# A second PSUM tile for the scores of batch 1, and batch 1 spread over one more H item, in a windowed attention followed by an MLP

## The chip, the cores and the metric

The kernel runs on one core of one Trainium2 chip. The metric is the device time in microseconds of one execution. A core has five engines that work side by side, each through its own list of instructions in order: PE (TensorE, matrix products and transposes into PSUM), ACT (ScalarE), DVE (VectorE), POOL (GpSimd) and SP (SyncE, which here only issues DMAs). [...] a matrix product writes a bank, and ACT or DVE must have read it before PE writes it again. An instruction that waits holds up everything behind it on its engine.

## The reference

Eight batches of eight heads with 576 positions and head size 64 go through causal attention with a window of 128 and an ALiBi bias; the heads are put side by side to 4608 tokens of 512, which go through two matrix products with a swish between them.

```python
scores = scale * np.matmul(q, k.transpose(0, 1, 3, 2))      # q, k, v: (8, 8, 576, 64)
mask = (rel >= 0) & (rel < 128)
scores = np.where(mask, scores + bias[None], -1000000000.0)
scores = scores - np.max(scores, axis=-1, keepdims=True)
attn = np.exp(scores)
attn = attn / (np.sum(attn, axis=-1, keepdims=True) + 1e-09)
attn_out = np.matmul(attn, v)
x = attn_out.transpose(0, 2, 1, 3).reshape(B * S, H * D)    # (4608, 512)
h = x @ w_in                                                # w_in: (512, 2048)
g = h * (1.0 / (1.0 + np.exp(-beta * h)))
out = g @ w_out                                             # w_out: (2048, 512)
```

## The kernel before, in words

**The steps of attention.** For a batch b, the first 512 positions of q and k are loaded for a pair of heads p and cast to bf16 by POOL (`load_pair`, line 113). `TP(b, p, i)` transposes q (i = 0) or k (i = 1) of that pair with four PE instructions (L224) into a `psum_t` bank, and DVE copies it to `QK` (L228). `TT(b)` does the same for the last 64 positions (L237, L242). `SC(b, m, p)` is a score step for one pair: it takes a PSUM tile of two banks, for batches 0 and 1 writes the bias into it with two products (L262), adds four (m = 0) or six (m = 1) products of q and k (L276), and ACT takes exp of the whole tile (L284). From batch 2 on the bias sits in four exps (L289) and DVE multiplies with a mask (L293); the masks and the exps' bias column are made by `late_consts` (L195, L200). `PV(b, qb, g)` multiplies the weights of query block qb and four heads g with v (L316, L320) and DVE divides by the sum (L325 reciprocal, L326 multiply). `X(b, qb)` transposes the finished 128 tokens with four PE instructions (L344), and ACT copies them into `XT`, the input of the MLP (L348); from batch 3 on a DMA does this.

**The steps of the MLP.** Tokens are taken in nine groups g of 512. `HS(g, j)`, an H item, is four products for 128 of the 2048 hidden columns (L360); ACT takes tanh (L365) and DVE makes `gT` of it (L366). `OS(g, i, n)` adds four of the sixteen products of an output block (L376), and after the last ACT scales it (L391) and a DMA stores it.

**PSUM.** `psum_s` holds one score tile (two banks), `psum_t` two banks for transposes, PV and X. In the first stage `psum_x` has the other four as two more score tiles. Then `psum_h` and `psum_o` take two banks each. `psum_o` is O's: it holds the output blocks, the first of which comes after H group 1. Before that it serves some H items and some PV steps.

**The order.** PE's order is written out by hand. Batch 0 runs first, then H group 0 begins: items 0 and 1, X(0, 4), items 2 to 7. Then `spread` lays all steps of batch 1 (`by_pair(1)`) evenly between items 8 to 13, in the order of that list: after each H item as many steps as its share of the cost. Items 14 and 15 with X(1, 2) and X(1, 3) follow, then batch 2's first transposes and group 1. The other engines follow PE's order as the framework places them; from group 1 on the orders of SP and POOL are fixed too. W1 (`moe_w_in`) comes in four chunks of 512 columns, so that H item 8 is the first that needs the third chunk and item 12 the first that needs the fourth.

```python
s1 = by_pair(1) + [pv(1, 3, 1)]
spread(h0[8:14], s1, 0, [(6, len(s1))])
h0[14]()
X(1, 2)
h0[15]()
X(1, 3)
```

Of the kernel before, what the change touches and what calls it, by code (L numbers as in the profile page):

```python
# [12 lines left out]
F32 = mybir.dt.float32  # L13
P = 128
# [3 lines left out]
def kernel(  # L18
# [10 lines left out]
    nc = tc.nc  # L29
# [12 lines left out]
    NQB = 5  # L42
    ROWS = [P, P, P, P, 64]
    NDM = DM // P
    NFF = DFF // P
# [28 lines left out]
    XT = const.tile([P, NDM, XTR], BF16, name="XT")  # L74
# [11 lines left out]
    psum_s = ctx.enter_context(tc.tile_pool(name="psum_s", bufs=1, space=bass.MemoryType.PSUM))  # L86
# [123 lines left out]
    def idle(to, n):  # L210

        for _ in range(n):
            nc.tensor.matmul(
                to, lhsT=zero[:, 0:P], rhs=zero[:], start=True, stop=True, skip_group_check=True
            )
# [4 lines left out]
    def TP(b, p, i):  # L220
        src = staged[b, p]
        tps = psum_t.tile([P, LA, P], BF16, name="tps", tag="t")
        for a in range(LA):
            nc.tensor.transpose(  # L224
                out=tps[:, a, :], in_=src[:, i, a, :, :].rearrange("r h d -> r (h d)"),
                identity=ident[:],
            )
        nc.vector.tensor_copy(  # L228
            out=QK[b % 2][:, i, p, 0:LM].rearrange("c (r a) -> c r a", a=LA),
            in_=tps[:].rearrange("c a r -> c r a"),  # L230
        )
# [100 lines left out]
    def X(b, qb):  # L332
        nq = ROWS[qb]
        xnv = xns.pop((b, qb))[:].rearrange("p h d -> p (h d)")
        tok0 = (b * S + P * qb) % XTR
        n1 = min(nq, XTR - tok0)
        parts = [(tok0, 0, n1)] + ([(0, n1, nq)] if n1 < nq else [])
        if b >= NTE:
            for at, r0, r1 in parts:
                nc.sync.dma_start_transpose(out=XT[:, :, at : at + r1 - r0], in_=xnv[r0:r1, :])  # L340
            return
        xt = psum_t.tile([P, NDM, P], BF16, name="xt", tag="t")
        for c in range(NDM):
            nc.tensor.transpose(  # L344
                out=xt[:, c, :], in_=xnv[:, c * P : (c + 1) * P], identity=ident[:]
            )
        for at, r0, r1 in parts:
            nc.scalar.copy(out=XT[:, :, at : at + r1 - r0], in_=xt[:, :, r0:r1])  # L348


    gts, opss = {}, {}

    def HS(g, j):
        if j == 0:
            gts[g] = gt_pool.tile([P, NFF, TOKG], BF16, name="gT", tag="gT")
        c0 = (g * TOKG) % XTR
        pool, tag = (psum_o, "ops") if j % 2 and j < (6, NFF - 1, 0)[min(g, 2)] else (psum_h, "hps")
        hps = pool.tile([P, TOKG], F32, name="hps", tag=tag)
        for c in range(NDM):
            nc.tensor.matmul(  # L360
                hps[:], lhsT=W1[:, c, bass.ts(j, P)], rhs=XT[:, c, c0 : c0 + TOKG],
                start=(c == 0), stop=(c == NDM - 1),
            )
        sig = sig_pool.tile([P, TOKG], BF16, name="sig", tag="sig")
        nc.scalar.activation(out=sig[:], in_=hps[:], func=ACTF.Tanh, scale=beta_h[:, j : j + 1])  # L365
        nc.vector.scalar_tensor_tensor(  # L366
            out=gts[g][:, j, :], in0=sig[:], scalar=1.0, in1=hps[:], op0=ALU.add, op1=ALU.mult
        )
# [73 lines left out]
    def step(f, c):  # L442
        cost[f] = c
        return f
# [5 lines left out]
        return step(lambda: TT(b), 1)  # L450

    def sc(b, m, p):
        return step(lambda: SC(b, m, p), 2)

    def pv(b, qb, g):

        pool = (psum_o, "ops") if b == 1 and (qb + g) % 2 and qb < 4 else None
        return step(lambda: PV(b, qb, g, pool), 1)

    def x(b, qb):  # L460
        f = step(lambda: X(b, qb), int(b < NTE))
        at[b, qb] = f
        if b >= NTE:
            lazy.append(f)
        return f

    at, lazy = {}, []
# [58 lines left out]
    with tc.manual_schedule(engines={mybir.EngineType.PE}):  # L526

        for sb in range(NQB):
            c = load_v(0, sb)()
            if sb in (1, 3):  # L530
                with tc.issue_after(c.ins):
                    for n in ((0,), (1, 2))[sb // 2]:
                        load_w1(n)
        for p in range(NP):
            c = load_pair(1, p, None if p else VS[0][0:1, NQB - 1, 0, 0:1])
            if p == 1:
                with tc.issue_after(c.ins):
                    load_w1(3)
                load_tail(1)
        for sb in range(NQB):  # L540
            c = load_v(1, sb)()
            if sb == 3:
                with tc.issue_after(c.ins):
                    for n in range(4):
                        load_w2(n)
        with tc.tile_pool(name="psum_x", bufs=2, space=bass.MemoryType.PSUM) as psum_x:
            pools = [psum_x, psum_s, psum_x]

            def sc0(m, p, fill=0):
                SC(0, m, p, pools[0], fill)  # L550
                pools.append(pools.pop(0))

            w = psum_t.tile([P, 512], F32, name="w", tag="t")
            idle(w[:], 9)
            TP(0, 0, 0)
            TP(0, 0, 1)
            sc0(0, 0, 3)
            load_beta()
            TP(0, 1, 0)
            TP(0, 1, 1)  # L560
            sc0(0, 1, 2)
            TT(0)
            TP(0, 2, 0)
            sc0(1, 0, 1)
            TP(0, 2, 1)
            sc0(1, 1)
            TP(0, 3, 0)
            sc0(0, 2)
            TP(0, 3, 1)
            sc0(1, 2)  # L570
            PV(0, 0, 0)
            sc0(0, 3)
            PV(0, 1, 0)
            sc0(1, 3)
            for qb in (2, 3):
                PV(0, qb, 0)
        psum_h = ctx.enter_context(
            tc.tile_pool(name="psum_h", bufs=2, space=bass.MemoryType.PSUM))
        psum_o = ctx.enter_context(
            tc.tile_pool(name="psum_o", bufs=2, space=bass.MemoryType.PSUM))  # L580
        w = psum_s.tile([P, 2, 512], F32, name="w", tag="sps")
        for qb in range(NQB - 1):
            c = PV(0, qb, 1, (psum_o, "ops") if qb % 2 else (psum_h, "hps"))
            idle(w[:, 0, :], 1)
            if qb:
                X(0, qb - 1)
                idle(w[:, 1, :], 1)
        X(0, NQB - 2)
        for g in range(2):
            c = PV(0, NQB - 1, g)  # L590
        with tc.issue_after(c.ins):
            late_consts()
        for p in range(NP):
            load_pair(2, p)
            if p == 1:
                load_tail(2)

        def hs(g):
            return [lambda j=j: HS(g, j) for j in range(NFF)]


        h0, at0 = hs(0), x(0, 4)
        for it in h0[0:2] + [at0] + h0[2:8]:
            it()
        s1 = by_pair(1) + [pv(1, 3, 1)]
        spread(h0[8:14], s1, 0, [(6, len(s1))])
        h0[14]()
        X(1, 2)
        h0[15]()
        X(1, 3)  # L610

        s2 = by_pair(2)
        for f in s2[0:2]:
            f()
        steps, first = [pv(1, 4, 1)] + s2[2:5] + [x(1, 4)] + s2[5:] + [x(2, 2)], {}
        for b in range(NTE, B):
            first[b] = len(steps)
            steps += by_block(b)
        steps += [pv(B - 1, 2, 1), x(B - 1, 2), pv(B - 1, 3, 1), x(B - 1, 3), pv(B - 1, 4, 1),
                  x(B - 1, 4)]  # L620
        with tc.manual_schedule(engines={mybir.EngineType.SP, mybir.EngineType.Pool}):

            early = [(0, 0), (1, 0), (0, 1), (1, 1), (0, 2), (1, 2)]
            late = [(0, 3), (1, 3)] + [(i, n) for i in (2, 3) for n in range(4)]

            def os(g, order):
                return [lambda i=i, n=n: OS(g, i, n) for i, n in order]

            todo, goals = merge(steps, first), []
            moe = hs(1) + os(0, early + late) + os(1, early)  # L630
            for g in range(2, NTG):
                b, r = divmod(TOKG * (g + 1) - 1, S)
                goals.append((len(moe) - 10, todo.index(at[b, r // P]) + 1))
                o = os(g - 1, late) + (os(g, early) if g < NTG - 1 else [])
                h = hs(g)
                moe += sum(([h[n]] + o[n : n + 1] for n in range(NFF)), [])
            spread(moe, todo, 2, goals)
            while stores:
                flush()
            for it in os(NTG - 1, early + late):  # L640
                it()
# [30 lines left out]
```

## Time and profile before

| | before |
|---|---|
| median of 8 executions | 338.62 us (337.82 to 339.56) |
| the profiled execution, its own time | 339.56 us |
| its span, first to last instruction | 337.4 us |
| PE busy | 319.2 us, 95% of the span |
| ACT busy | 215.8 us, 64% |
| DVE busy | 192.2 us, 57% |
| POOL busy | 107.0 us, 32% |
| tensor clock granted | 1.00 of full speed |
| DMA | 48.26 MB, mean 143 GB/s |

The times in the profile count from the first instruction of the profiled execution. A row of the timeline or of the instruction groups names start, busy time, engine, source line, operation and the tiles written and read; the bracket at its end tells how long the engine sat idle before it and what ended that wait. A row of the waits gives the total, the number of times and the longest one. Consecutive instructions of one engine overlap a little, so the start-to-start distance, not the busy time, is what one more of them costs.

### The profile page before, as it was taken

What the parts mean: (1) busy time and instruction counts of PE and PEld (TensorE: products, weight loads), DVE (VectorE), ACT (ScalarE), POOL (GpSimd) and SP (SyncE); (2) the same over time, 40 slices, a digit from 0 to 9 for tenths busy, and PEclk for the clock granted to TensorE, in tenths of its full rate; (3) what the DMA queues carried; (4) which work ended last, traced back from release to release, by engine and by line L of the source; (5) the groups of instructions that cost most, each with busy time, mean ns of one, the idle gap of its engine ahead of it and who ended that gap; (6) DMA issues with size and microseconds to landing.
All of it is one profiled execution on the core that took longest, in us unless ns stands there. A gap on an engine that the chain in (4) does not pass through costs nothing.

```text
span 337.4 us, 6166 instructions
## 1 busy us (share of the span) xinstructions
PE 319.2 (95%) x2240; PEld 152.3 (45%) x2283; DVE 192.2 (57%) x412; ACT 215.8 (64%) x417; POOL 107.0 (32%) x173
## 2 busy tenths in 40 slices
PE   8987787999999999999999999999999999999895
PEld 3453344444544444444444444444444444444342
DVE  6676756797435575656666665566656455344500
ACT  5755466697647876776687757776676664354611
POOL 7742592273553434524243243520100001010000
PEclk9999999999999999999999999999999999999999
DMA  8999989999999999899989788990402012110011
GB/s 199 247 174 243 213 212 234 225 185 170 224 209 213 137 190 182 192 137 201 141 193 176 141 134 183 191 148 12 102 31 64 1 64 62 39 64 31 32 64 62
DMA packets 138638, 48.26 MB, mean 143 GB/s; under 512 B 125664, under 2 KB 136176, under 8 KB 138608
## 3 DMA queue, kind: packets, MB, share of 16 engines
q1 hardware_dynamic: 108208, 32.19, 51.2%
q0 software_dynamic: 30224, 15.54, 33.9%
q8 instruction: 18, 0.29, 0.4%
q10 hardware_dynamic: 176, 0.14, 0.1%
q14 instruction: 12, 0.10, 0.1%
HBM read 36.71 MB, written 9.44 MB: 137 GB/s over the span
## 4 chain that ended last, share of the span: by engine, by line
PE 83%; DMA 7%; DVE 3%; ACT 2%; SPq 1%; issue 1%; POOL 0%
PE ops L376 37%; PE hps L360 34%; PE sps L276 5%; DMA W<-in_moe_w_in_dram 4%; PE pv L320 2%; PE pv L316 2%; DMA fst<-in_k_dram 2%; DMA fst<-in_v_dram 2%; DVE gT L366 1%; PE sps L262 1%; SPq L109 1%; ACT pt L284 1%; ACT sig L365 1%; PE tps L224 1%; DVE qkT L228 1%
## 5 line engine op out<-in xcount | busy, mean ns | idle before, releaser
L360 PE MATMUL hps<-XT,W 128*128 128x512 bf16 x555 | 143.6, 379 | 4.9 <-DMA W<-in_moe_w_in_dram 2.2
L365 ACT ACTIVATE sig<-hps,beta_h 128x512 bf16<-128x512 f32 x144 | 99.2, 692 | 71.9 <-PE hps L360 64.3
L376 PE MATMUL ops<-W,gT 128*128 128x512 bf16 x558 | 142.5, 379 | 1.2 <-issue 0.3
L366 DVE SCALAR_TENSOR_TENSOR gT<-sig,hps 128x512 bf16<-128x512 bf16 x144 | 98.2, 683 | 54.3 <-ACT sig L365 53.6
L289 ACT ACTIVATE pt<-sps,bias 128x256 bf16<-128x256 f32 (+1 forms) x192 | 75.1, 479 | 10.4 <-PE sps L276 10.3
L360 PEld LDWEIGHTS <-W 128*128 128x128 bf16 x576 | 52.1, 98 | 62.0 <-issue 5.0
L376 PEld LDWEIGHTS <-gT 128*128 128x128 bf16 x576 | 51.2, 97 | 55.7 <-issue 2.1
L293 DVE TENSOR_TENSOR pt<-pt,mask 128x1024 bf16<-128x1024 bf16 x48 | 35.5, 740 | 43.9 <-ACT pt L289 43.9
L394 POOL DMA_DIRECT2D out_dram<-osb x32 | 17.9, 560 | 130.1 <-ACT osb L391 130.1
L129 POOL CAST bst<-fst 128x512 bf16<-128x512 f32 (+1 forms) x50 | 31.7, 645 | 42.2 <-DMA fst<-in_q_dram 30.7
L326 DVE TENSOR_TENSOR xn<-pv,zs 128x256 bf16<-128x256 f32 (+1 forms) x80 | 33.6, 422 | 2.3
L391 ACT ACTIVATE osb<-ops 128x512 f32<-128x512 f32 x35 | 21.0, 601 | 18.1 <-PE ops L376 18.0
L320 PE MATMUL pv<-vs,pt 128*128 128x65 bf16 x320 | 28.1, 193 | 0.0
L320 PEld LDWEIGHTS <-pt 128*128 128x128 bf16 x320 | 21.5, 97 | 10.2 <-issue 0.9
L276 PE MATMUL sps<-qkT 64*128 64x256 bf16 (+2 forms) x320 | 25.2, 252 | 0.5 <-DVE qkT L228 0.2
L325 DVE RECIPROCAL zs<-pv 128x4 f32<-128x4 f32 (+1 forms) x80 | 13.8, 174 | 19.4 <-PE pv L320 19.2
L316 PE MATMUL pv<-vs,pt 128*128 128x65 bf16 x256 | 23.5, 193 | 0.6 <-ACT XT L348 0.5
L284 ACT ACTIVATE pt<-sps 128x1024 bf16<-128x1024 f32 x16 | 16.4, 1024 | 11.8 <-PE sps L276 11.4
L276 PEld LDWEIGHTS <-qkT 64*128 64x128 bf16 x320 | 10.4, 94 | 27.8 <-issue 26.3
L316 PEld LDWEIGHTS <-pt 128*128 128x128 bf16 x256 | 19.8, 98 | 6.7 <-issue 0.7
L137 POOL DMA_DIRECT2D vs<-in_v_dram x25 | 21.4, 859 | 0.9 <-issue 0.5
L113 POOL CAST bst<-fst 128x512 bf16<-128x512 f32 x24 | 14.6, 621 | 19.7 <-DMA fst<-in_q_dram 12.9
(47 smaller groups left out, 113.2 us busy)
## 6 DMA issues: line engine op xcount, KB each, us to landing
fst<-in_q_dram SPq DMA_DIRECT2D x32, 256.0 KB, 4.6
fst<-in_k_dram SPq DMA_DIRECT2D x32, 256.0 KB, 5.1
out_dram<-osb POOLq DMA_DIRECT2D x32, 256.0 KB, 3.0
fst<-in_v_dram SPq DMA_DIRECT2D x12, 256.0 KB, 6.6
vs<-in_v_dram POOLq DMA_DIRECT2D x20, 128.0 KB, 5.5
W<-in_moe_w_in_dram POOLq DMA_DIRECT2D x4, 512.0 KB, 8.5
W<-in_moe_w_out_dram POOLq DMA_DIRECT2D x4, 512.0 KB, 13.9
fst<-in_q_dram SPq DMA_DIRECT2D x8, 128.0 KB, 5.1
```

The source lines that it names most:

```text
L129: nc.gpsimd.tensor_copy(out=t[0 : ROWS[sb], i], in_=f)
L137: nc.gpsimd.dma_start(out=to, in_=v[b, :, P * sb : P * sb + ROWS[sb], :].rearrange("h p d -> p h d"))
L276: nc.tensor.matmul(o, lhsT=qk[64 * e : 64 * e + 64, 1, p, P * kb : P * kb + P], rhs=qk[64 * e : 64 * e + 64, 0, p, P * kb : P * kb + nq], ...
L289: nc.scalar.activation(out=pt[:, e, cols], in_=sps[:, e, cols], func=ACTF.Exp, scale=qscale, bias=bias[:, half, h : h + 1],)
L293: nc.vector.tensor_tensor(out=pt[:], in0=pt[:], in1=masks[m][:].rearrange("p (o c) -> p o c", o=1).broadcast_to([P, 2, 512]), op=ALU.mult,)
L316: nc.tensor.matmul(pv[:, hl, 0 : D + 1], lhsT=weights(b, qb - 1, h, 1), rhs=vs[:, qb - 1, h, 0 : D + 1], start=True, stop=False,)
L320: nc.tensor.matmul(pv[:, hl, 0 : D + 1], lhsT=weights(b, qb, h, 0), rhs=vs[:, qb, h, 0 : D + 1], start=qb == 0, stop=True,)
L326: nc.vector.tensor_tensor(out=xn[0:nq, 4 * g : 4 * g + 4, :], in0=pv[0:nq, :, 0:D], in1=zs[0:nq].broadcast_to([nq, 4, D]), op=ALU.mult,)
L360: nc.tensor.matmul(hps[:], lhsT=W1[:, c, bass.ts(j, P)], rhs=XT[:, c, c0 : c0 + TOKG], start=(c == 0), stop=(c == NDM - 1),)
L365: nc.scalar.activation(out=sig[:], in_=hps[:], func=ACTF.Tanh, scale=beta_h[:, j : j + 1])
L366: nc.vector.scalar_tensor_tensor(out=gts[g][:, j, :], in0=sig[:], scalar=1.0, in1=hps[:], op0=ALU.add, op1=ALU.mult)
L376: nc.tensor.matmul(ops_[:], lhsT=gT[:, j, i * P : i * P + P], rhs=W2[:, j, :], start=(j == 0), stop=(j == NFF - 1),)
```

## The change

There are four edits.

1. While batch 1 runs, the two banks that will be O's hold a second score tile (`psum_y`), and the score steps alternate between it and `psum_s`. Before that, the same two banks are `psum_z`, for odd H items of group 0 and for some PV steps of batch 0. `psum_o` is opened only after batch 1's spread. PV steps of batch 1, of which some had used `psum_o`, all use `psum_t` now.
2. Batch 1's steps are spread over H items 7 to 13 in place of 8 to 13, so that the first of them come before item 8.
3. `late_consts` is placed on DVE right after the first two transposes' copies, in place of after batch 0's last PV.
4. The copies of `X(1, ·)` into `XT` are made by DVE in place of ACT.

```diff
@@ TP
-        nc.vector.tensor_copy(
+        return nc.vector.tensor_copy(
@@ X
+        copy = nc.vector.tensor_copy if b == 1 else nc.scalar.copy
         for at, r0, r1 in parts:
-            nc.scalar.copy(out=XT[:, :, at : at + r1 - r0], in_=xt[:, :, r0:r1])
+            copy(out=XT[:, :, at : at + r1 - r0], in_=xt[:, :, r0:r1])
-    gts, opss = {}, {}
+    gts, opss, spare = {}, {}, {}
@@ HS
-        pool, tag = (psum_o, "ops") if j % 2 and j < (6, NFF - 1, 0)[min(g, 2)] else (psum_h, "hps")
+        pool, tag = psum_h, "hps"
+        if j % 2 and (g == 1 and j < NFF - 1 or "z" in spare):
+            pool, tag = spare.get("z") or psum_o, "ops"
@@ sc, pv
     def sc(b, m, p):
-        return step(lambda: SC(b, m, p), 2)
+        def f():
+            pool = None
+            if "y" in spare:
+                pool = spare["y"][0]
+                spare["y"].reverse()
+            SC(b, m, p, pool)
+
+        return step(f, 2)
     def pv(b, qb, g):
-        pool = (psum_o, "ops") if b == 1 and (qb + g) % 2 and qb < 4 else None
-        return step(lambda: PV(b, qb, g, pool), 1)
+        return step(lambda: PV(b, qb, g), 1)
@@ first stage
-            TP(0, 0, 1)
+            c = TP(0, 0, 1)
+            with tc.issue_after(c.ins):
+                late_consts()
@@ from batch 0's last steps to group 1
-        psum_o = ctx.enter_context(
-            tc.tile_pool(name="psum_o", bufs=2, space=bass.MemoryType.PSUM))
...
-        with tc.issue_after(c.ins):
-            late_consts()
+        h0, s1 = hs(0), by_pair(1) + [pv(1, 3, 1)]
+        with tc.tile_pool(name="psum_z", bufs=2, space=bass.MemoryType.PSUM) as psum_z:
+            spare["z"] = psum_z
...
+            for it in h0[0:2] + [x(0, 4)] + h0[2:7]:
+                it()
+            del spare["z"]
...
-        for it in h0[0:2] + [at0] + h0[2:8]:
-            it()
-        s1 = by_pair(1) + [pv(1, 3, 1)]
-        spread(h0[8:14], s1, 0, [(6, len(s1))])
+        with tc.tile_pool(name="psum_y", bufs=1, space=bass.MemoryType.PSUM) as psum_y:
+            spare["y"] = [psum_s, psum_y]
+            spread(h0[7:14], s1, 0, [(7, len(s1))])
+            del spare["y"]
+        psum_o = ctx.enter_context(
+            tc.tile_pool(name="psum_o", bufs=2, space=bass.MemoryType.PSUM))
         h0[14]()
```

More of the change, by code (lines that the diff above doesn't have):

```diff
@@ L578, with hs @@
             tc.tile_pool(name="psum_h", bufs=2, space=bass.MemoryType.PSUM))
-        psum_o = ctx.enter_context(
-            tc.tile_pool(name="psum_o", bufs=2, space=bass.MemoryType.PSUM))
[L581 to L590, printed above, removed]
-        with tc.issue_after(c.ins):
-            late_consts()
+        def hs(g):
+            return [lambda j=j: HS(g, j) for j in range(NFF)]
+        h0, s1 = hs(0), by_pair(1) + [pv(1, 3, 1)]
+        with tc.tile_pool(name="psum_z", bufs=2, space=bass.MemoryType.PSUM) as psum_z:
+            spare["z"] = psum_z
+            w = psum_s.tile([P, 2, 512], F32, name="w", tag="sps")
+            for qb in range(NQB - 1):
+                PV(0, qb, 1, (psum_z, "ops") if qb % 2 else (psum_h, "hps"))
+                idle(w[:, 0, :], 1)
+                if qb:
+                    X(0, qb - 1)
+                    idle(w[:, 1, :], 1)
+            X(0, NQB - 2)
+            for g in range(2):
+                PV(0, NQB - 1, g)
+            for it in h0[0:2] + [x(0, 4)] + h0[2:7]:
+                it()
+            del spare["z"]
         for p in range(NP):
@@ L596 @@
                 load_tail(2)
-        def hs(g):
-            return [lambda j=j: HS(g, j) for j in range(NFF)]
-        h0, at0 = hs(0), x(0, 4)
-        for it in h0[0:2] + [at0] + h0[2:8]:
-            it()
-        s1 = by_pair(1) + [pv(1, 3, 1)]
-        spread(h0[8:14], s1, 0, [(6, len(s1))])
+        with tc.tile_pool(name="psum_y", bufs=1, space=bass.MemoryType.PSUM) as psum_y:
[4 more added lines that the diff above has]
+            tc.tile_pool(name="psum_o", bufs=2, space=bass.MemoryType.PSUM))
         h0[14]()
```

## The prediction

> **What bounds the kernel now.** I read the busy time by stretch first, because a mean over the span hides where the tensor engine (PE) is not full.
>
> ```profile
> core 0: us, PE busy (x) PEld busy (x) DVE busy (x) ACT busy (x) POOL busy (x), PEclk, DMA share, GB/s
> ...
> 20.00:30.00 10.00, 9.62 (x78) 5.16 (x76) 7.57 (x32) 6.89 (x12) 0.93 (x2) 1.00 1.17 218
> 30.00:40.00 10.00, 5.71 (x49) 2.94 (x49) 6.35 (x12) 4.08 (x6) 6.08 (x10) 1.00 1.16 231
> 40.00:50.00 10.00, 8.39 (x79) 4.16 (x81) 5.00 (x14) 6.24 (x8) 7.41 (x12) 1.00 0.88 202
> 50.00:60.00 10.00, 8.09 (x95) 4.94 (x94) 6.49 (x17) 6.29 (x10) 2.54 (x5) 1.00 1.18 233
> 60.00:70.00 10.00, 9.36 (x70) 4.59 (x69) 8.22 (x15) 7.46 (x15) 4.01 (x6) 1.00 1.11 224
> 70.00:80.00 10.00, 9.89 (x79) 4.95 (x80) 9.97 (x19) 9.49 (x22) 5.88 (x9) 1.00 1.55 184
> ```
>
> From 70 to 300 us PE is about 99% busy at clock 1.00: PE is the bound there and a change of order gains nothing. The open time lies at 30 to 60 us, where 10 us slices hold 5.71, 8.39 and 8.09 of PE. That is batch 1 among H items 8 to 15 of group 0, exactly what the diff rearranges. The waits of PE in the window 28 to 75 us, longest first, say what ends its idle time:
>
> ```profile
> PE hps L360 <- DMA W<-in_moe_w_in_dram: 2.2, 1, 2.2
> PE tps L224 <- DVE qkT L228: 2.0, 3, 0.8
> PE sps L262 <- ACT pt L284: 1.9, 3, 0.9
> PE tps L224 <- ACT XT L348: 0.8, 1, 0.8
> PE tps L224 <- DVE xn L326: 0.6, 1, 0.6
> ```
>
> H item 8 stands behind item 7 and waits 2.2 us for the third chunk of W1; transposes wait for the two `psum_t` buffers; a score step waits until the exp has left the only score tile. The timeline gives the arrivals that nothing in the diff moves (POOL casts end where bf16 data is ready):
>
> ```profile
> 32.58 1.04 PE L360 MATMUL hps<-XT,W 128*128 128x512 bf16 x4 [2.22 <-DMA W<-in_moe_w_in_dram]
> 32.92 0.61 POOL L113 CAST bst<-fst 128x512 bf16<-128x512 f32 x1 [1.17 <-DMA fst<-in_k_dram]
> 35.32 2.62 POOL L113 CAST bst<-fst 128x512 bf16<-128x512 f32 x4
> 41.93 0.61 POOL L142 CAST vs<-fst 128x512 bf16<-128x512 f32 x1 [3.25 <-DMA fst<-in_v_dram]
> 47.32 0.59 PE L262 MATMUL sps<-table,sident 128*128 128x512 bf16 x2 [0.88 <-ACT pt L284]
> 52.24 1.04 PE L360 MATMUL hps<-XT,W 128*128 128x512 bf16 x4
> 58.38 0.38 PE L224 MATMUL tps<-ident,bst 128*128 128x128 bf16 x4 [0.81 <-ACT XT L348]
> ```
>
> k of pair 1 is cast by 33.53; pairs 2 and 3 by 35.95, 36.6, 37.3 and 37.94; v block 1 by 42.54. H item 13 begins at 52.24, and the second transpose of batch 2 at 58.38, just ahead of group 1.
>
> **The change, part by part.** The queues of POOL and SP issue the same instructions in the same order, and up to the batch-2 loads none of those waits for PE work that is moved, so I keep all arrivals. PE issues the same matmuls. Prices, from back-to-back starts in the timeline: H item 0.87 us, score step 0.85, TP 0.22, TT 0.44, PV 0.22 (0.13 for query block 0), X 0.22; exp 1.03 on ACT, tanh 0.6; on DVE gT 0.6 in a row, TP copy 0.6, reciprocal plus multiply 0.57.
>
> *One H item earlier in the spread.* Item 7 ends at 30.37 as before. Now the four transposes of pairs 0 and 1 and score (0,0) come before item 8. TP(1,0,·) run 30.37 to 30.82 and TP(1,1,0) at 31.8 (q cast 31.75), then PE waits for k: TP(1,1,1) at 33.57. Score (0,0) ends 34.64, item 8 ends 35.5. Its W1 wait is gone, since the chunk landed at 32.5, but 1.6 us of it comes back as the wait for k. Before, score (0,0) ended at 36.89 with item 8 done: the lead is 1.4 us.
>
> *Second score tile.* Following PE on, each step at the latest of engine, data and buffer: TP(1,2,0) 35.97 (cast), TP(1,2,1) 36.62 (cast), score (0,1) to 37.7, item 9 to 38.57, TP(1,3,·) to 39.0, score (0,2) to 39.9, TT to 40.3, item 10 to 41.2, PV(1,0,0) to 41.3, score (0,3) to 42.15. PV(1,1,0) waits for v: 42.57. Then without a wait: score (1,0) to 43.6, item 11 to 44.5, PV(1,0,1), score (1,1) to 45.5, PV(1,1,1), item 12 to 46.6, score (1,2) to 47.4, X(1,0), PV(1,2,0), score (1,3) to 48.7, item 13 from 48.7 to 49.6. Each tile's exp ended before its next use: (0,2) at 40.9 for a use at 42.8, (1,0) at 44.8 for 46.6, (1,1) at 46.6 for 47.9. Item 13 ended at 53.1 before, so the lead is 3.5 us.
>
> *PV back in `psum_t`, X copies on DVE.* This is what it pays with. Between item 13 and group 1 nine fills (X, PV 3/0, 4/0, 2/1, 3/1, X, X, TP, TP) share two banks, all drained by DVE in a fixed order: X copy, reciprocal (3,0), gT 13, multiply (3,0), and so on. gT 13 stands ahead of that multiply and waits for tanh 13, which follows the last exp (49.8): it runs 50.55 to 51.2, so the multiply ends 51.5 and PV(1,2,1), which needs that bank, starts at 51.6. PV(1,3,1) follows at 52.1, item 14 ends 53.2, X(1,2) 53.4, item 15 54.3, X(1,3) 54.5, its copy 55.0, second TP of batch 2 at 55.05 (before: 58.38). The lead at group 1 is 3.3 us.
>
> The X copy is an operation whose row is on another engine. On ACT it takes 578 ns (L348, 128x512). DVE's nearest rows have the same 512 bf16 elements out of PSUM: 420 ns where both sides run in unbroken rows (L242), 684 ns where one is strided (L228). [...] The X output runs unbroken for 128 tokens, so I take 0.42, L242's row. By 0.69, three copies on this chain and the queue behind them put the second TP at 55.8 and the lead at 2.6; I keep both.
>
> *Constants early.* 18 instructions, 2 x 0.27 and 1.04 for sixteen: 1.6 us of DVE, from 6.97. DVE is idle there for 1.26 us before `beta_h` (8.23), so the next qkT copies slip by 0.1 to 0.3 and the score step at 9.90, which waited 0.20 for such a copy, with them. This is covered by the 1.5 us wait for k before 33.57; without it, the cost is 0.3. Where they stood (23.25) PE waited for nothing, so nothing is gained there.
>
> *Costed at nothing.* The pools that follow each other on the same banks: the last reader before the new score tile is gT 5 (done by 30.1), first use 36.8; the last exp in it ends 49.8, the next use is H item 1 of group 1 after 55. Were it otherwise, one exp, 1.03. X(1,4) on DVE (about 0.3): DVE was idle 0.77 before 66.73; without that, 0.3. ACT loses 2.7 us that PE waited for only once (0.81).
>
> *Afterwards.* Batch 2 arrives by itself (last k cast 63.33, its TP at 71.29: 8.0 spare), W2's first use is at 77.56 and its last load has landed by 65.2 (issued 46.6, at most 18.6 to landing). Batch 3's first score (93.70) needs block transposes that SP issues until 84.64 and that land 5.4 later (median of those issued at 82 to 85 us): 3.7 spare. 3.3 fits in all.
>
> Sum: 339.56 (span 337.4 plus 2.2 around it) less 3.3 is 336.3 for the profiled execution. That one stood 0.94 above the median of the runs; the same 3.3 off 338.62 gives **335.3 us**.
>
> **Rivals.**
> (1) Part is given back: the X copy at 0.69 (lead 2.6), the batch-3 transposes landing in 6.3, the longest of 80 to 90 us (90.9, with the score wanted at 90.4: 0.5), handoffs of 0.05 that I rounded off at some 16 places (0.8). Together the gain is 1.3, 337.3. For it: DVE is 9.97 of 10 busy at 70 to 80. Against: the three need not fall together.
> (2) The gain vanishes: data, not PE, sets group 2 and later, as the DMA share over 1 in 50 to 130 us allows; then 338.6. Against it: PE shows one wait of 0.6 at 60 to 82 us and no DMA wait at all after 33.
> (3) Slower: `psum_t` becomes the bound. If each of the nine fills had to wait for a drain with a gT ahead of it, at 0.57 plus 0.6 a fill costs 1.17, nine cost 10.5 in place of 5.28 from the end of item 13 to the second TP: 5.2 lost against 3.5 won, 340.3. It decides from 0.98 us a fill on ((5.28 + 3.5) / 9). For it: the fixed DVE order, and PV's two extra banks are given up. Against: only gT 13 and gT 14 lie among the nine.
> (4) The edit doesn't do what it says: if the second tile's scores still waited for the preceding exp, three waits come back, 1.9, leaving 1.4: 337.2. The order of the built instructions alternates the tiles, so this is part of (1)'s chance.
>
> **How the numbers follow.** About 0.3% (1.0 us) is what a measurement of this kernel can tell from no change. Forecast with a gain of 2.3 to 4.3: 0.62. More than that, should the arrivals I wait for (k, v) come earlier: 0.06. Rivals (1) and (4), gain 1.0 to 2.3: 0.18. Rival (2): 0.08. Rival (3): 0.06. Faster 0.86, same 0.08, slower 0.06. The range reaches from a gain of 4.7 to one of 1.3: 333.9 to 337.3.
>
> **What would show it.** Right: no PE wait for W1; a wait for the k cast ahead of the fourth transpose, about 1.5; no L262 wait for exp; one wait for v near 42; item 13 at 48.7 and group 1 at 55.3; the 30 to 60 us slices nearer 7, 9.5 and 9; X copies on DVE at 0.42. Wrong: PV or transposes waiting for DVE over 2 us in all between 49 and 56, or score steps of batch 3 waiting for a DMA near 90.

## The result and the profile after

The changed kernel takes 335.23 us, the median of 11 executions (334.02 to 337.26), against 338.71 for the kernel before (32 executions): the ratio is 0.9902, with a 95% interval of 0.9885 to 0.9920. The forecast was 335.3 us, a gain of 3.3; the measured gain is 3.5. Another set of executions, beside other kernels, gave 335.26 and 0.9899 (0.9874 to 0.9925). The profiled execution is one of 335.23 us with a span of 333.2, so it stands at its own median, while that of before (339.56) stood 0.9 above its own; the two profiled spans therefore differ by more (4.2) than the medians do.

The busy time by stretch of the changed kernel (PE is the first pair after the length of the stretch, DVE the third, ACT the fourth):

```profile
30.00:40.00 10.00, 8.25 (x73) 4.50 (x73) 8.21 (x14) 5.72 (x8) 6.02 (x10) 1.00 1.20 247
40.00:50.00 10.00, 9.34 (x106) 4.87 (x106) 6.46 (x18) 7.80 (x10) 7.94 (x13) 1.00 1.01 218
50.00:60.00 10.00, 8.37 (x74) 4.83 (x76) 8.87 (x21) 4.12 (x6) 2.57 (x5) 1.00 1.19 231
```

PE gained where the edits are: 5.71 became 8.25 and 8.39 became 9.34 (the prediction's sign was about 7, 9.5 and 9). The slice from 50 to 60 hardly moved (8.09 to 8.37) although it now reaches further into group 1. In it DVE rose from 6.49 to 8.87. The waits of PE from 28 to 75 us, all of them:

```profile
PE tps L224 <- DVE qkT L228: 1.6, 2, 0.8
PE pv L316 <- DVE xn L326: 0.7, 1, 0.7
PE tps L224 <- DVE xn L326: 0.6, 1, 0.6
PE tps L224 <- DVE XT L349: 0.3, 1, 0.3
PE pv L316 <- DVE XT L349: 0.3, 1, 0.3
```

The W1 wait (2.2) and the exp waits (1.9) are gone. What is left are 3.5 us of waits for one engine, DVE, which has to empty the two `psum_t` banks; the 0.6 among them, in batch 2, was there before. The timeline shows where the others lie, and the landmarks of the forecast:

```profile
31.57 0.68 DVE L228 COPY qkT<-tps 128x512 bf16<-128x512 bf16 x1
31.75 0.62 POOL L113 CAST bst<-fst 128x512 bf16<-128x512 f32 x1 [0.44 <-DMA fst<-in_k_dram]
32.17 0.68 DVE L369 SCALAR_TENSOR_TENSOR gT<-sig,hps 128x512 bf16<-128x512 bf16 x1
32.30 0.38 PE L224 MATMUL tps<-ident,bst 128*128 128x128 bf16 x4 [0.79 <-DVE qkT L228]
33.50 0.38 PE L224 MATMUL tps<-ident,bst 128*128 128x128 bf16 x4 [0.81 <-DVE qkT L228]
39.37 1.03 PE L363 MATMUL hps<-XT,W 128*128 128x512 bf16 x4
47.65 1.04 PE L363 MATMUL hps<-XT,W 128*128 128x512 bf16 x4
49.43 0.19 PE L316 MATMUL pv<-vs,pt 128*128 128x65 bf16 x1 [0.27 <-DVE XT L349]
50.53 0.20 PE L316 MATMUL pv<-vs,pt 128*128 128x65 bf16 x1 [0.70 <-DVE xn L326]
54.17 0.38 PE L224 MATMUL tps<-ident,bst 128*128 128x128 bf16 x4 [0.30 <-DVE XT L349]
54.39 2.75 PE L363 MATMUL hps<-XT,W 128*128 128x512 bf16 x12
```

The fourth transpose starts at 33.50 (forecast 33.57), but it waits for a bank, not for k, which was cast by 32.37. Item 13 starts at 47.65 (forecast 48.7, before 52.24), the second transpose of batch 2 at 54.17 (forecast 55.05, before 58.38). H items 8 and 9 start at 34.57 and 36.74, H item 10 at 39.37, group 1 at 54.39 (before 58.60). The waits for DVE between item 13 and group 1 add up to 1.27 us, under the 2 us that the prediction named as a sign of being wrong. From there on to the end, PE waits for no DMA.

### The profile page after: what moved, and what is told of

It reads as the page before. It is cut to its first block, busy times and chain, and to the rows that moved or that the text cites. A ratio compares the mean times of both kernels' runs of the same rounds, so it can differ in the third digit from the quotient of the medians.

```text
span 333.2 us, 6165 instructions
## 1 busy us (share of the span) xinstructions
PE 318.9 (96%) x2240; PEld 152.3 (46%) x2283; DVE 194.0 (58%) x417; ACT 213.7 (64%) x412; POOL 106.3 (32%) x173
## 4 chain that ended last, share of the span: by engine, by line
PE 88%; DMA 4%; DVE 3%; ACT 2%; SPq 1%; issue 1%; POOL 0%
PE ops L379 38%; PE hps L363 37%; PE sps L276 6%; PE pv L320 3%; PE pv L316 2%; DMA fst<-in_q_dram 2%; DMA fst<-in_v_dram 2%; DVE gT L369 1%; ACT sig L368 1%; PE xt L344 1%; PE sps L262 1%; SPq L109 1%; PE tps L224 1%; DVE xn L326 1%; SPq L95 0%
## 5 line engine op out<-in xcount | busy, mean ns | idle before, releaser
L293 DVE TENSOR_TENSOR pt<-pt,mask 128x1024 bf16<-128x1024 bf16 x48 | 34.7, 722 | 43.3 <-ACT pt L289 43.3
L320 PE MATMUL pv<-vs,pt 128*128 128x65 bf16 x320 | 28.4, 193 | 0.3 <-POOL vs L142 0.3
L316 PE MATMUL pv<-vs,pt 128*128 128x65 bf16 x256 | 24.1, 193 | 1.4 <-DVE xn L326 0.7
```

Source lines behind the costliest of these rows:

```text
L293: nc.vector.tensor_tensor(out=pt[:], in0=pt[:], in1=masks[m][:].rearrange("p (o c) -> p o c", o=1).broadcast_to([P, 2, 512]), op=ALU.mult,)
L316: nc.tensor.matmul(pv[:, hl, 0 : D + 1], lhsT=weights(b, qb - 1, h, 1), rhs=vs[:, qb - 1, h, 0 : D + 1], start=True, stop=False,)
L320: nc.tensor.matmul(pv[:, hl, 0 : D + 1], lhsT=weights(b, qb, h, 0), rhs=vs[:, qb, h, 0 : D + 1], start=qb == 0, stop=True,)
```

## The experiments

All times are medians; each ratio compares all the kernel's executions with those of the kernel before on the same chip, so it can differ a little from the ratio of the medians. First every part of the change was taken back alone, then three parts were put alone into the kernel before, then the changed kernel was rearranged. Rows of the form "PE ... <- ..." are out of the waits of PE from 28 to 75 us (total, times, longest); rows that begin with a time are out of the timeline.

Two stretches tell more than the totals, because they depend little on when the loads arrive. All figures are from one start to the next in the profiles, in us:

| from the start of H item 10 to that of item 13, same order of PE | |
|---|---|
| one score tile (second tile taken back; spread alone) | 9.99, 9.99 |
| two score tiles (changed kernel, twice; constants back; X on ACT; end rearranged) | 8.28, 8.11, 8.10, 8.48, 8.54 |

| from the start of H item 13 to that of group 1 | |
|---|---|
| before; spread alone; constants alone | 6.36 in all three |
| all PV of batch 1 in `psum_t`, X copies on DVE (changed kernel, twice; spread, tile or constants back; start rearranged) | 6.73 to 6.74 in all six |
| all PV of batch 1 in `psum_t`, X copies on ACT (X copies back; second tile alone) | 7.27 in both |
| end of batch 1 rearranged (three kernels) | 6.40 in all three |

### Taking one part back

**Spread.**

```diff
-            for it in h0[0:2] + [x(0, 4)] + h0[2:7]:
+            for it in h0[0:2] + [x(0, 4)] + h0[2:8]:
...
-            spread(h0[7:14], s1, 0, [(7, len(s1))])
+            spread(h0[8:14], s1, 0, [(6, len(s1))])
```

> The changed kernel, but with batch 1 spread over H items 8 to 13 again. Theory A (the gain is the sum of two removed waits, W1 for item 8 and exp for the single score tile): the 1.4 us lead of the earlier start is lost, up to 2.2 where W1 lands late: 336.6 to 337.4 us, with a PE wait for W1 of 1 to 2 us ahead of item 8. Rival B (the stage is set by DVE and the arrivals of k and v, so the W1 wait is filled again later): within 0.3 us of the changed kernel, 335.2.

Measured: 336.71 us, ratio 0.9929 (0.9903 to 0.9955), 1.5 slower than the changed kernel by the medians, 0.9 by the ratios. In its timeline the W1 wait is back ahead of item 8:

```profile
31.54 1.04 PE L363 MATMUL hps<-XT,W 128*128 128x512 bf16 x4 [1.75 <-DMA W<-in_moe_w_in_dram]
```

The median is theory A's, and group 1 begins 1.07 us later (55.46) than in the changed kernel. The intervals of the two kernels overlap, so the wait is shown and the size is not.

**Second tile.**

```diff
-            spare["y"] = [psum_s, psum_y]
+            spare["y"] = [psum_s, psum_s]
```

> The changed kernel, but with every score step in psum_s; the second tile is there and unused. Theory A: the exp waits come back (three of 0.4 to 0.9 us before, 1.9 in all): 336.9 to 337.4 us. Rival B (the v casts and DVE order set item 13): under 0.5 us lost, 335.7 or less.

Measured: 337.02 us, ratio 0.9949 (0.9928 to 0.9970), 1.8 slower than the changed kernel by the medians, 1.6 by the ratios: theory A. Its exp waits are fewer than in the kernel before (1.1 in place of 1.9, two in place of three), and yet item 13 begins 1.9 us later than in the changed kernel, at 49.58:

```profile
PE sps L262 <- ACT pt L284: 1.1, 2, 0.6
39.59 1.03 PE L363 MATMUL hps<-XT,W 128*128 128x512 bf16 x4
42.62 0.59 PE L262 MATMUL sps<-table,sident 128*128 128x512 bf16 x2 [0.57 <-ACT pt L284]
48.72 0.59 PE L262 MATMUL sps<-table,sident 128*128 128x512 bf16 x2 [0.55 <-ACT pt L284]
```

H item 10 begins only 0.22 later than in the changed kernel (39.59 against 39.37; the casts of pair 2 came later here), so 1.71 of the 1.93 arise between items 10 and 13, where both exp waits lie. With one tile this stretch takes 9.99 in both kernels that have it, with two 8.1 to 8.5: the tile is worth 1.5 to 1.9 us there, and rival B is out. The two listed waits are 1.1 of that; what makes up the rest the list does not show.

**X copies.**

```diff
-        copy = nc.vector.tensor_copy if b == 1 else nc.scalar.copy
+        copy = nc.scalar.copy
```

> The changed kernel, but with the copies of X(1, .) on ACT again. Theory A (nine fills of two banks after item 13, drained by DVE, set the start of group 1): each copy costs 0.16 more on ACT but leaves DVE's queue, where two of them stand ahead of what PE waits for; within 0.4 us of the changed kernel, 334.8 to 335.6. Rival D (ACT, with the exps and tanh, is what the move relieves): 0.6 to 1 us slower, 335.8 to 336.2, with PE waiting for the ACT copy for about 0.8.

Measured: 336.30 us, ratio 0.9932 (0.9906 to 0.9959), 1.1 slower by the medians, 1.0 by the ratios, though the intervals overlap. The median is a little above rival D's range, and the waits are rival D's. Two waits for the ACT copy stand in its timeline:

```profile
49.19 1.04 PE L363 MATMUL hps<-XT,W 128*128 128x512 bf16 x4
51.50 0.19 PE L316 MATMUL pv<-vs,pt 128*128 128x65 bf16 x1 [0.81 <-ACT XT L349]
56.24 0.38 PE L224 MATMUL tps<-ident,bst 128*128 128x128 bf16 x4 [0.70 <-ACT XT L349]
56.46 2.75 PE L363 MATMUL hps<-XT,W 128*128 128x512 bf16 x12
```

X(1, 1)'s copy stands behind tanh 13 and the last exp on ACT (in the kernel before, exp from 52.35, tanh from 53.32, copy from 53.90), and PV(1, 4, 0) needs its bank. The start of item 13 to the start of group 1 took 7.27 us here (49.19 to 56.46) and 6.74 in the changed kernel (47.65 to 54.39): 0.53. The same two figures come back in every other profile with the same PV banks (second table above), so these 0.5 us are the copy's place; they lie between theory A and rival D. The rest of the 1.1 lies ahead of item 13, where this execution's casts came later, and isn't shown to be the edit's.

**Constants.**

```diff
-            c = TP(0, 0, 1)
-            with tc.issue_after(c.ins):
-                late_consts()
+            TP(0, 0, 1)
...
-                PV(0, NQB - 1, g)
+                c = PV(0, NQB - 1, g)
+            with tc.issue_after(c.ins):
+                late_consts()
```

> The changed kernel, but with the exp constants made where they were, after batch 0's last PV. Theory A (their 1.6 us are covered in both places): 335.2, within 0.3. Rival C (in the changed kernel's profile the two masks took 0.90 us together beside POOL's casts, in place of 0.54, and H item 0 began at 23.77 in place of 23.06: the early constants delay the first stage): 0.5 to 0.7 us faster than the changed kernel, 334.6, with H item 0 near 23.1.

Measured: 335.75 us, ratio 0.9912 (0.9885 to 0.9938): not told apart from the changed kernel. H item 0 began at 23.87, later than the 23.1 that rival C wanted; rival C's 334.6 is below the interval.

### One part alone in the kernel before

**Spread alone** (`h0[2:7]`, then `spread(h0[7:14], s1, 0, [(7, len(s1))])`).

> The kernel before with one edit alone: batch 1 spread over H items 7 to 13 in place of 8 to 13. Theory A (two separate waits, each removed by its own edit): the W1 wait of 1.7 to 2.2 us goes, the exp waits (1.9) and the wait for the ACT copy of X stay: 336.7 to 337.4, that is 1.3 to 2.0 faster than before. Rival B (a lead ahead of a single score tile is spent waiting for its exp, so the edits only work together): under 0.7 us faster, 338.0 or more.

Measured: 336.79 us against 339.20 beside it, ratio 0.9940 (0.9920 to 0.9960): 2.0 to 2.4 faster, at or above the top of theory A's range and far from rival B. But theory A had the exp waits stay, and the spread by itself halves them (1.9 to 0.9). That H items then stand between other steps may be the reason; it isn't shown:

```profile
PE sps L262 <- ACT pt L284: 0.9, 2, 0.5
```

Nor does the gain hang on the W1 wait. In the profile of the constants alone (below), which starts batch 1 behind item 8 like the kernel before, W1 came in time: group 1 began at 56.84 in place of 58.60. With the spread alone it began at 54.92, still 1.9 earlier, with H item 0 at nearly the same time (22.97 and 22.91). Against that profile the spread saves 0.6 of a wait for gT, 1.0 of exp waits and 0.4 of waits for the `psum_t` banks, and loses 0.2 to a cast of v.

**Second tile alone** (with `psum_z` and `psum_y` as in the change and all PV of batch 1 in `psum_t`; spread, constants and X copies as before).

> The kernel before with the second score tile alone, and what comes with it (all PV of batch 1 in psum_t); the spread from item 8, the late constants and X copies on ACT are as before. Theory A (tile worth about 1.8 where the rest is changed, its price in psum_t under 0.5): 1.3 to 1.8 us faster than before, 337.0 to 337.5. Rival G (with X on ACT the two psum_t banks eat it: the changed kernel with X on ACT was 1.1 us slower than with X on DVE): 0.7 or less faster, 338.1 or more.

Measured: 336.80 us against 339.06, ratio 0.9942 (0.9920 to 0.9964): 2.0 to 2.3 faster. Theory A's side, with somewhat more than it said. Item 8 started right behind item 7 in this profile and waited for no W1, so the tile's gain doesn't come from that wait. But the run changes one thing more: H item 7 falls into `psum_z` here, so item 8 needs no bank that gT 6 has to empty. In the profile of the constants alone item 8 waited 0.64 for it. Up to some 0.6 us of this gain can be that bank's and not the score tile's; in the changed kernel item 7 is in `psum_h`. (With the spread taken back, item 7 is in `psum_z` too, but there item 8 waited longer for W1.)

**Constants alone.**

> The kernel before with one edit alone: the exp constants made early. Theory A (1.6 us of DVE covered in both places): no change, 338.4 to 339.1, within 0.3 of before. Rival C (over the nine profiles so far H item 0 began at 22.5 to 24.4 us, later on the mean with early constants, so they delay the first stage): 0.4 to 0.7 us slower than before, H item 0 at 23.5 to 23.8.

Measured: 338.77 us against 339.06, ratio 0.9990 (0.9974 to 1.0006); H item 0 at 22.91. No effect; rival C is out. All its other waits are those of before, apart from W1's: here item 8 waited 0.64 for DVE's gT in place of 2.2 for W1.

```profile
PE hps L360 <- DVE gT L366: 0.6, 1, 0.6
```

The single gains add to more than the whole: 0.60% for the spread, 0.58% for the tile, 0.30% for X (from taking it back) make 1.5%, where the change brings 1.0%. Spread and tile remove partly the same exp waits: the spread alone leaves 0.9 of the 1.9.

### Can the remaining DVE waits be removed?

**End of batch 1.**

```diff
...
+            if "y" in spare and (qb, g) in ((4, 0), (2, 1)):
+                pool = (psum_s if g == 0 else spare["all"][1], "sps")
...
         h0[14]()
-        X(1, 2)
         h0[15]()
+        X(1, 2)
         X(1, 3)
```

> The changed kernel with the fills after item 13 rearranged: PV(1, 4, 0) goes to psum_s and PV(1, 2, 1) to psum_y, which are free after the last exps, and items 14 and 15 both come before X(1, 2) and X(1, 3). Theory A (in the changed kernel the two psum_t banks cost three waits of 0.7, 0.3 and 0.3 us between item 13 and group 1): about 1.0 to 1.3 us faster than the changed kernel, 334.0 to 334.3. Rival E (DVE itself, 8.87 of 10 busy at 50 to 60 us, sets the start of group 1, whichever bank is filled): within 0.3, 335.0.

Measured: 336.08 us against 339.20, ratio 0.9901 (0.9871 to 0.9930): by the ratio no different from the changed kernel, which is rival E's forecast; its median is 0.9 higher. With two more banks, PE comes earlier and waits for DVE under other names (two waits for POOL's casts, 0.3 and 0.2, lie ahead of that):

```profile
PE xt L344 <- DVE xn L326: 0.8, 1, 0.8
PE tps L224 <- DVE XT L349: 0.5, 1, 0.5
PE hps L363 <- DVE gT L369: 0.3, 1, 0.3
```

Item 13 to group 1 took 6.40 us (48.60 to 55.00) in place of 6.74. The 0.34 is the same in all three kernels that have this end, but the waits listed in the stretch still add up to 1.28 (0.75 and 0.53). Theory A's 1.0 or more is out.

**Start of batch 1**: the transposes of pair 0 ahead of item 7, those of pair 1 behind it, then item 8; PV(1, 1, 0) one score step later.

```diff
-            sc(b, 0, 3), pv(b, 1, 0), sc(b, 1, 0), pv(b, 0, 1), sc(b, 1, 1), pv(b, 1, 1),
+            sc(b, 0, 3), *([sc(b, 1, 0), pv(b, 1, 0)] if b == 1 else [pv(b, 1, 0), sc(b, 1, 0)]),
+            pv(b, 0, 1), sc(b, 1, 1), pv(b, 1, 1),
...
-            for it in h0[0:2] + [x(0, 4)] + h0[2:7]:
+            for it in h0[0:2] + [x(0, 4)] + h0[2:7] + s1[0:2] + h0[7:8] + s1[2:4]:
...
-            spread(h0[7:14], s1, 0, [(7, len(s1))])
+            spread(h0[8:14], s1[4:], 0, [(6, len(s1) - 4)])
```

> The changed kernel with another start of batch 1: the transposes of pair 0 before H item 7, those of pair 1 after it, then item 8 and the first score; and PV(1, 1, 0) one score step later, because its v block is cast only at 41.4 us. Theory A (in the changed kernel four transposes in a row wait 1.6 us for the two psum_t banks, and an H item between two pairs hides it): 0.8 to 1.0 us faster than the changed kernel, 334.3. Rival F (arrivals set the pace: q and k of pair 1 are cast at 31.3 and 32.4, pairs 2 and 3 up to 36.8, v from 41.4): the lead is spent waiting for casts, within 0.3, 335.0.

Measured: 335.55 us against 339.20, ratio 0.9896 (0.9873 to 0.9920). Not told apart from the changed kernel: rival F. One of the two 0.8 waits for DVE is gone; in its place PE waits for POOL's casts of pair 2 (0.17 and 0.21). No wait for v of 0.15 or more stands in batch 1.

**Both.**

> Both rearrangements, of the start and of the end of batch 1, in the changed kernel. Theory A: the gains add, 1.8 to 2.3 us faster than the changed kernel, 333.0 to 333.4. Rivals E and F: the work of DVE and the arrivals bound the stage, under 0.6 us, 334.7 or more.

Measured: 334.87 us against 339.20, ratio 0.9879 (0.9855 to 0.9903), between the theories; its interval overlaps the changed kernel's. POOL's casts of pair 2 now hold PE at the start:

```profile
PE tps L224 <- POOL bst L113: 0.8, 2, 0.5
```

**Both, with batch 1's tail loaded and cast behind pairs 2 and 3.** In the kernels so far POOL worked through the tail casts (1.17 us in the changed kernel) ahead of pair 2, though PE needs the tail only after pairs 2 and 3.

```diff
             if p == 1:
                 with tc.issue_after(c.ins):
                     load_w1(3)
-                load_tail(1)
+        load_tail(1)
```

> Both rearrangements of batch 1 as before, and the tail of batch 1 (its last 64 positions) loaded and cast after pairs 2 and 3 in place of ahead of them. Theory F (POOL's casts, in order with 1.17 us of tail casts and a DMA issue ahead of pair 2, hold the transposes of pair 2 once the start is rearranged: PE waited 0.8 to 1.2 for them): 0.5 to 1.0 us faster than without, 333.9 to 334.4. Rival H (what is won there is waited for at the v casts from 41.4 on, or DVE sets the end): within 0.3 of it, 334.9.

Measured: 333.87 us (333.42 to 334.36, 5 executions), ratio 0.9854 (0.9833 to 0.9876): the time is theory F's, and this is the fastest kernel of this study. The two intervals overlap, so that the last edit alone brought the 1.0 is not shown by the times; PE's wait for POOL is gone from the profile. In it item 13 starts at 46.33 and group 1 at 52.73:

```profile
PE tps L224 <- DVE qkT L228: 0.8, 1, 0.8
PE xt L344 <- DVE xn L326: 0.8, 1, 0.8
PE tps L224 <- DVE xn L326: 0.6, 1, 0.6
PE tps L224 <- DVE XT L349: 0.5, 1, 0.5
PE hps L363 <- DMA XT<-xn: 0.6, 1, 0.6
```

The last row, out of the waits of PE from 75 us to the end (it lies at 131 us), is new: in the kernel with the largest lead an H item waits for the DMA that fills `XT` from batch 3 on. From group 1 to the end this profile takes 279.6 us in place of 278.8, so its lead is no longer kept whole.

**The changed kernel once more**, beside the last three:

> The changed kernel itself once more, beside the others on the same chip: 335.2, 3.5 us faster than before, so that the rearranged one can be held against it directly; both theories expect the same.

Measured: 335.26 us (334.82 to 336.69, 6 executions), ratio 0.9899. The rearranged kernel is 1.4 us faster, and its slowest execution is faster than the fastest of these.

## Why the prediction was right

**The bound.** The forecast that only 30 to 60 us is open, and that the lead at group 1 lasts to the end, held. The span to go from the start of group 1 was 278.8 us before (337.4 less 58.60) and is 278.8 after (333.2 less 54.39); the repeat of the changed kernel has 279.3, at a granted clock of 0.998. Rivals (1) and (2) asked for waits of batch 3 on DMAs or of group 2 on data; there is none. Rival (1)'s copy at 0.69 took 0.42.

**The tile.** The exp waits went as said, and the stretch from item 10 to item 13 shows the tile's worth: 1.5 to 1.9 us. Rival (4), a second tile that brings nothing, is out.

**The spread.** The W1 wait went as said, but that is not the whole of the gain. The spread alone brought some 2 us, and in profiles without a wait for W1 it still put group 1 1.9 earlier. The working priced it by the W1 wait alone (2.2, of which 1.6 comes back). The single gains, some 2 us each, add to more than the whole; the working met this rightly by following all parts together and not adding two wait totals.

**The k wait.** This step failed. The working held the casts of pair 1 where they had been and let PE wait 1.0 us for q and, up to 33.53, 1.5 for k. In the changed kernel's execution k was cast by 32.37, H item 7 ended 0.7 later, and the wait of 1.6 was for the two `psum_t` banks, with gT 6 and gT 7 among DVE's copies. Size and place agree by luck: the term was an arrival out of a single execution, and the waits for the banks, which the prediction had read in the kernel before (2.0 in all), lie hidden behind those casts in the working. Over the fourteen profiles the same k cast ended anywhere between 30.9 and 33.5. The casts of pairs 2 and 3 came 1.2 earlier too: item 8 ended where the working had it (35.44 against 35.5), item 9, behind two transposes that the working let wait for these casts, began 0.96 ahead of it (36.74 against 37.7), and item 13 1.05. The wait for v that was forecast near 42 is not among the waits either.

**The price in `psum_t`.** Waits were forecast for X(1, 1)'s copy, for the multiply (3,0) behind gT 13, and for X(1, 3)'s copy; from the starts in the working I make them some 0.3, 1.0 and 0.3. The trace has 0.27, 0.70 and 0.30. From the end of item 13 to the second transpose of batch 2 the working gave 5.45 us and the trace has 5.65, against 5.27 before. Rival (3) named the right place, but its fill costs 0.63 us (5.65 over 9), under the 0.98 from which it would decide. Banks are only part of the cause, as the rearranged end shows: with two more banks and another order the stretch is 0.34 shorter, and PE still waits 1.28 us there for DVE (0.75 and 0.53).

**The X copy.** The row chosen, L242 with its 420 ns, was the right one: DVE took 422 ns for what ACT took 578. The instruction groups show it:

```profile
L349 DVE COPY XT<-xt 128x512 bf16<-128x512 bf16 x4 | 1.7, 422 | 1.4 <-PE xt L344 1.4
```

What ACT is relieved of was put at nothing, because PE had waited for its copies only once (0.81). That reading missed a second wait in the same stretch, 0.30 for PV(1, 3, 1) at 54.53, and the working never asked what these waits become once all PV are in `psum_t`: with the copies on ACT that stretch takes 7.27 us, with DVE 6.74. The move is worth 0.5 there; the rest of the 1.1 by the medians is open.

**The constants.** Costed at nothing, and no cost shows: alone they gave 0.9990 (0.9974 to 1.0006). The cover that was named for them, the wait for k, was not there.

**Profile against median.** That the median came out within 0.1 us of the forecast is in part luck. The forecast took the same 3.3 off profile and median; the profiled executions differ by 4.3, the medians by 3.5. Against the working, the changed kernel's profile was 0.9 ahead at group 1, with casts earlier than assumed. And in the kernel before the W1 wait, 2.2 in its profile, was absent in the profiles of two other kernels that start batch 1 behind item 8; it comes and goes with the arrivals, so a profile above its median is likely to hold more of it. This last step is argued from four profiles and not settled.

## What to carry to other kernels

Follow all parts of a change through one hand-made timetable, each step at the latest of engine, buffer and data: waits removed by different edits overlap, and their totals must not be added. Treat an arrival read from one profile as a range of a microsecond or two (the k cast here ended between 30.9 and 33.5), and ask which wait stands behind it. To tell an edit from the arrivals, compare the length of a stretch that begins after them, over several kernels. When a buffer's drain is late, see what else stands ahead of it on the draining engine before giving it another buffer; and when PE waits for a cast, look at what less urgent work the casting engine does first.

## What the runs showed of the hardware

A copy of 128x512 bf16 from PSUM to SBUF took DVE 422 ns with unbroken rows (L349, changed kernel) and 684 with a strided side (L228, kernel before), and ACT 578 (L348, kernel before).

The two mask instructions of 128x512 bf16 took DVE 0.26 and 0.28 us in the kernel before. Made early, they took 0.48 or 0.49 us together in six profiles, and 0.59, 0.62, 0.69 and 0.90 in the four others. With the spread taken back they ran from 6.67 for 0.48, and POOL's cast began as they ended, at 7.14, and took 0.61. In the changed kernel they ran from 6.88 for 0.90, and the cast began 0.05 after them and took 0.71. So in that profile, where they ran side by side, both were longer; no run isolates the cause.

Over the fourteen profiles H item 0 began between 22.5 and 24.4 us, whether the constants were early (22.50 to 24.36) or late (22.97 to 23.88).
